# An attention and MLP block written out by a planner: first norm, Q lead, leftover cost, token order and bias row changed together

## The chip, the core and the metric

The kernel runs on one core of one Trainium2 chip. The metric is device time in microseconds (us). The core has five engines with queues of their own: PE (matrix multiply), DVE (vector), ACT (activation functions), POOL (general purpose) and SP, which here issues nearly all DMAs. Each engine works through its own instructions in the order in which the program lists them.

## The reference

One transformer block with modulation by a condition c, on 2048 tokens of width 512, with 32 heads of 16 columns and an MLP of width 1376:

```python
mod = (_silu(c) @ w_mod).reshape(c.shape[0], 6, 1, -1)      # sa, ca, ga, sb, cb, gb
h = _layernorm(x) * (1 + ca) + sa
q, k, v = split(h @ wqkv)                                   # 32 heads of 16
p = _softmax(q @ k.T * 16 ** -0.5)
x = x + ga * ((p @ v) @ wo)
h = _layernorm(x) * (1 + cb) + sb
x = x + gb * (_gelu(h @ w1 + b1) @ w2 + b2)
```

All inputs are bf16. The scores are 32 heads x 2048 x 2048 numbers, and each of them has to pass through an exponential: this is most of the work outside the matrix engine.

## The kernel before

**Blocks, runs and tiles.** Tokens are worked in four blocks of 512 (NQ, QB), each of four tiles of 128 (TPB). A head group is 8 heads, 128 columns of Q, K and V (index cc); the pair (b, cc) is a Q block with a head group. Attention is cut into 32 runs. A run handles four heads of one query block (in the last block, eight heads for half of the queries) and goes over 16 key tiles. A key tile of a run has four score units, one for each row group of 32 partitions of PE; a unit is 128x512 scores, made by one matmul in `qk` (L856). Two runs share one Q group; the Q tiles (`qm`) have four buffers.

**Two ways to the exponential.** ACT takes three or two units at a time from the PSUM tiles `st` and writes `pt` (L905). For up to four key tiles of each run (DKS; one in the first run) DVE takes the units instead, from the PSUM tiles `ax`: it writes score bits as 16-bit integers into `ph` (L946), which read as bf16 are a coarse exponential. Five readings with shifted bits, each against a V scaled to suit (VEB and the four VX of a tile), are added up by PE to refine it. The second to fourth readings are three adds on DVE (L962). The fifth, `shared_reading`, is four pieces; POOL takes as many as fit (L984), and DVE does the leftover in one instruction (L978) of 512 to 2048 columns. If a run's own tiles are used up, ACT takes from the tiles that DVE has not reached.

**Values.** `pv_op` (L1044) multiplies exponentials or readings with V and adds a run up in the PSUM bank `od`. After a run, `normalise` copies it out (L1069), and turns sums into reciprocals over small DMAs (dn, dc, rn, RB, issued on SP).

**The planner.** The order on every engine is written out by a planner in Python, before the program is built. Each piece of work is an `op` with an engine, a cost in us, what it depends on, a priority and at times a due point. `Plan.step` starts the piece that can start first; among those of an engine that can start nearly together it takes the lowest priority number, plus a small hashed amount (`spread`) that depends on the line or kind of the piece and on a seed, which changes every 25 us of planned time. Planned costs decide only the order; the hardware then goes by semaphores. When PE would have too little to do, the planner adds matmuls on zeros (L465, L470, L481) to keep it busy.

**Start.** SP issues the first x tile in two halves, two column blocks of w_mod, then (after the first of those has landed) the weight columns of the first head group, the other x tiles and the remaining columns. `layer_norm` works on DVE: statistics (`stats`, L641 and L642), POOL takes the power -1/2 (`rstd`, L646 and L648), DVE applies it (`apply`, L652), PE transposes (L694). In the first block the result is modulated as it is read from the PSUM tiles `st`, by DVE (L660) and ACT (L657). modA, the modulation, is made on PE from w_mod (L617) and finished on DVE (L630, L631). Then `make_q` (masked on DVE, L753), `make_k` (evicted by ACT, L665) and `make_v` (DVE, L667), with the projections at L735 and L774.

**Later Q groups.** `qk_deps` calls `want_q` whenever it lists a score matmul, and that makes the Q group needed next: four matmuls (L735), an eviction to `qs` on DVE (L757), and eight DMAs of 16 KB each, issued by SP (L763), that spread the heads into `qm`.

**Tails.** When the last run of a block is done, `block_tail` does the output projection, the second norm, W1, one tanh-approximated Gelu over the block on ACT (L1286, between two table loads) and W2 (L1210). The bias b2 is a row of the third part of W2 (`W2c`), met by rows of ones in `g`, which POOL writes after the Gelu (`ones`, L1217). W2 is scaled by the gate gb on POOL (L1119). The last block is done in halves; `last_half` follows the last exponential.

Of the kernel before, what the change touches and what calls it, by code (L numbers as in the profile page):

```python
# [11 lines left out]
ACT = mybir.ActivationFunctionType  # L12
# [51 lines left out]
SEEDS = (327, 149, 358, 994, 115, 625, 198, 230, 172, 718, 221, 116, 464, 544, 26, 159, 31, 414, 105, 313, 53, 464, 554, 383, 223, 329, 85, 286, 52, 14, 445, 498)  # L64
HEAT = 1.5

# [40 lines left out]
class Plan:  # L107
# [51 lines left out]
    def spread(self, o):  # L159
        x = ((sum(map(ord, o.kind)) if o.eng == "PE" else o.fn.__code__.co_firstlineno if o.fn else 0) * 2654435761 ^ SEEDS[min(int(self.now // 25.0), len(SEEDS) - 1)] * 2246822519) & 0xFFFFFFFF  # L160
        x = ((x ^ x >> 15) * 2246822519) & 0xFFFFFFFF
        return SPREAD * ((x ^ x >> 13) & 1023) / 1024.0
# [120 lines left out]
def kernel(  # L283
# [28 lines left out]
    EPS = 1e-5  # L312
    QSC = 0.25 * 128.0 / math.log(2.0)
# [95 lines left out]

    APR = 32  # L410
# [77 lines left out]
    x_src = A_x[0].rearrange("(b t p) d -> b p t d", t=TPB, p=P)  # L488
# [24 lines left out]
    def v_cols(v):  # L513
        return v[:, 0:32 * VW].rearrange("p (h w) -> p h w", w=VW)
# [8 lines left out]
    def load_x(b, deps=()):  # L523
        def go(o):
            nc.sync.dma_start(out=o.tile, in_=x_src[b])
        return dma(go, deps, kb=512, acq=r_xb, prio=0.0)
# [7 lines left out]
    for h in range(2):  # L534
        o_x0 += 2 * [dma(lambda o, h=h: nc.sync.dma_start(out=o_x[0].tile[:, 2 * h:2 * h + 2, :],
                                                         in_=x_src[0][:, 2 * h:2 * h + 2, :]),
                         (o_x[0],), kb=256, prio=0.0)]
    first = {}

    def load_mod(i):  # L540
        def go(o):
            first[i] = nc.sync.dma_start(out=o.tile, in_=wm_src[:, :, i * D:(i + 1) * D])
        return dma(go, kb=512, acq=r_blk, prio=0.01 + 0.01 * i)
    o_wm = {i: load_mod(i) for i in (0, 1)}

    def behind(i, load):
        tc.add_manual_dep(load.ins, first[i].ins.name, mybir.DependencyInfo(
            mybir.DependencyClass.Sync, mybir.DependencyReason.DATA), reason="order of loads")
    o_w, o_w0 = {}, {}
# [3 lines left out]
    def load_cols(i, lo, hi, prio):  # L553
        def go(o):
            got = nc.sync.dma_start(out=o_w[i].tile[:, :, lo:hi], in_=wq_src[:, :, i * D + lo:i * D + hi])
            if lo == 0 and i == 0:
                behind(0, got)
        return dma(go, (o_w[i], o_wm[0]), kb=(hi - lo) * (2 if lo == 0 else 1), prio=prio, n=2.7)
    o_w0 = {i: load_cols(i, 0, P, 0.1 + 0.01 * i) for i in range(3)}
    o_w1 = {}  # L560
    for b in range(1, NQ):
        o_x[b] = load_x(b, (o_wm[0],))
        o_x[b].prio = 0.2 + 0.1 * b
        o_w1[b - 1] = load_cols((1, 2, 0)[b - 1], P, D, 0.25 + 0.1 * b)
# [58 lines left out]
    def mod_columns(dst, ws, kind, warmer=True):  # L623
# [5 lines left out]
        def out_(o):  # L629
# [4 lines left out]
    o_mA = mod_columns(modA, [(o_wm[i], lambda i=i: o_wm[i].tile, o_wm[i]) for i in range(2)],  # L634
                       "modA", False)


# [6 lines left out]
    def rstd(ln, lo, hi):  # L644
        mv, rs = ln.tile
        nc.gpsimd.tensor_scalar(out=rs[:, lo:hi], in0=mv[:, lo:hi, 1], scalar1=EPS, scalar2=None,  # L646
                                op0=ALU.add)
        nc.gpsimd.tensor_tensor(out=rs[:, lo:hi], in0=rs[:, lo:hi], in1=mhalf[:, lo:hi], op=ALU.pow)  # L648
# [20 lines left out]
    def layer_norm(src, deps, mod, mod_dep, hold_z, alloc_h, engines, ps_res, kind, prio,  # L669
# [3 lines left out]
        st = [op("DVE", lambda o, t=t: stats(ln, t, src(t)), 0.83, (deps[t], ln, after and after[t]), prio=prio)  # L673
              for t in range(nt)]
        rs = [op("POOL", lambda o, i=i: rstd(ln, 2 * i, 2 * i + 2), 1.3,
# [49 lines left out]

    o_h = {}
# [7 lines left out]
    def proj(b, w, cc, kind, acq, after=None):  # L734
        return chain([(lambda ps, j=j: nc.tensor.matmul(  # L735
            out=ps[:, 0:QB], lhsT=w.tile[:, j, cc * P:(cc + 1) * P], rhs=o_h[b].tile[:, j, :],
            start=(j == 0), stop=(j == NC - 1)), MM) for j in range(NC)],
            [w, (o_w1 if cc else o_w0)[[o_w[i] for i in range(3)].index(w)], after] + (o_hd[b] if b else []), kind, acq, (o_h[b], w),
            need=None if b else lambda j: o_hd[b][j])

# [30 lines left out]
    def make_v(b, cc, kind, acq, eng, after=None):  # L771
# [14 lines left out]
        for t in DKS:  # L786
            if t // TPB == b:
                def scale(o, t=t):
                    for ph in range(1, NPH):
                        nc.gpsimd.tensor_scalar(  # L790
                            out=v_cols(VX[(t, ph)])[:, 8 * cc:8 * cc + 8, 0:16],
                            in0=v_cols(v_tile(t, 0))[:, 8 * cc:8 * cc + 8, 0:16], scalar1=PH_W[ph],
                            scalar2=0.0, op0=ALU.mult, op1=ALU.add)
                got.append(op("POOL", scale, 4 * 0.3, [got[0]] + o_vx0[t], prio=1.0, port=True))
# [66 lines left out]
    def qk_deps(r, kt):  # L861
        want_q(r // 2 + 1 if r < LAST * 8 else r - LAST * 4 + 2)
        cc, par, hb = run_heads(r)
        qm, evs = o_q[(cc, runs[r][0])]
        return [evs[par or 0], o_k[(cc, kt // TPB)]], qm
# [102 lines left out]
    def shared_reading(r, kt, first, es):  # L968
# [18 lines left out]
        def part(o):  # L987
            after_dve(add_pairs())
            n_piece[0] += 1
            if todo:  # L990
                done.todo += 1
            else:
                drop()
            o.waiters.append(done)
# [128 lines left out]
    def w2_scaled():  # L1123
        return scaled([lambda f=f: W2[f // 4].tile[:, f % 4, :] if f < 8 else W2c[:, f - 8, :] for f in range(NF)],
                      gb_bc, (W2[0], W2[1], o_late["small"], o_late["gb"]))
# [20 lines left out]
    def late_loads(after):  # L1146
# [11 lines left out]
        def wo(o):  # L1158
            nc.sync.dma_start(out=Wo, in_=A_wo.rearrange("(c p) f -> p c f", p=P))
            wo_src = A_wo[(NC - 1) * P:NC * P, :].rearrange("(r p d) f -> r p d f", r=4, p=2)  # L1160
            for r in range(4):
                for p in range(2):
# [4 lines left out]
                                   nc.gpsimd.memset(b1_bf, 0.0),  # L1167
# [48 lines left out]
    def ones(g, deps):  # L1216
        return op("POOL", lambda o: nc.gpsimd.memset(g.tile[FL:P, NF - 1, :], 1.0), 0.4, deps, prio=0.0)  # L1217
# [22 lines left out]
    def block_tail(b, nt=TPB):  # L1240
# [19 lines left out]
        if part:  # L1260
            g.uses += 1
            x2.uses += 1
            held["x"] = x2
            o_late["part"] = g
            one = ones(g, (g,))
# [19 lines left out]
        else:  # L1285
# [3 lines left out]
            one = ones(g, ge)  # L1289
# [17 lines left out]
    def store(b, t, a):  # L1307
        dma(lambda o: nc.sync.dma_start(
            out=out[0][b * QB + t * P:b * QB + (t + 1) * P, :], in_=a.tile), (a,), kb=128, rel=(a,))
# [94 lines left out]
    for b in range(NQ):  # L1404
        kind = f"in{b}"
        urgent.add(kind)
        o_h[b], o_hd[b], za, trs = layer_norm(
            lambda t, b=b: o_x[b].tile[:, t, :], o_x0 if b == 0 else [o_x[b]] * TPB, modA, o_mA, prev_tr, r_blk,
            ("DVE", "ACT") * 2 if b == 0 else ("DVE", "DVE", "ACT", "ACT") if b < 3 else ("DVE",) * 4, tuple(r_st[::-1]) if b == 0 else (r_ax, r_ax), kind, 0.6 + 0.2 * b, after)
# [8 lines left out]
        make_k(b, 0, kind, r_ax, "ACT")  # L1418
# [16 lines left out]
    def want_q(g):  # L1435
        while q_made[0] < g and q_made[0] + 1 < NQ * NC:
            q_made[0] += 1
            b, cc = groups[q_made[0]]
            due(32 + APR * (first_run(q_made[0]) - 1) - 32)
# [97 lines left out]
```

## Time and profile before

| what | value |
|---|---|
| runs | 781.15, 783.46, 783.68 us; median 783.46 |
| span of the profiled execution, first to last instruction | 782.9 us |
| first exponential (L905) starts | 14.79 us |
| ACT busy | 752.0 us, of which the exponentials 710.7 in 626 instructions |
| DVE busy | 722.6 us, of which the first readings (L946) 315.8 in 484 instructions |
| PE busy | 730.8 us |
| POOL busy | 256.6 us |
| DMA | 27.71 MB in 38547 packets, mean 35 GB/s |
| mean granted TensorE clock | 0.993 |

The time that the profiled execution took as a run is not listed beside its span; the span lies 0.56 us below the median of the runs, and within their spread. Times inside the profile count from the first instruction. A line such as L905 is a line of the kernel's source. "out<-in" gives the names of the tiles, and after the bar stand the busy time in us, the mean duration in ns, the idle time of the engine just before and what ended it.

### The profile page before, as it was taken

How to read it: one execution, taken by the hardware profiler on the slowest of the kernel's cores; microseconds unless marked ns; L12 is line 12 of the kernel's file. 1: busy time of each engine (PE TensorE's matmuls, PEld its weight loads, DVE VectorE, ACT ScalarE, POOL GpSimd, SP SyncE). 2: the span in 40 equal slices, each digit the busy share in tenths (PEclk: the TensorE clock that was granted, in tenths of full speed). 3: DMA queues.
4: the chain of work that ended last, by engine and by line, in shares of the span. 5: the costliest groups of instructions: out<-in, count | busy, mean ns of one | idle time of the engine just before them, and what ended most of it. 6: DMA issues, size and time to landing. Idle time of an engine off the chain costs nothing.

```text
span 782.9 us, 20900 instructions
## 1 busy us (share of the span) xinstructions
PE 730.8 (93%) x8315; PEld 271.3 (35%) x8395; DVE 722.6 (92%) x1269; ACT 752.0 (96%) x677; POOL 256.6 (33%) x492
## 2 busy tenths in 40 slices
PE   8889999999999999999999999999999999999997
PEld 3323333233333222233223233332333444444444
DVE  6789989999999999999999999999987999998984
ACT  4999999999999999999999999999999999999994
POOL 6620434333352534231313134234202432142320
PEclk9999999999999999999999999999999999999999
DMA  7043001100002001000101000000110000100000
GB/s 216 28 147 83 18 23 43 27 23 5 17 21 75 25 17 49 17 13 15 47 19 30 29 19 17 20 22 19 29 57 24 23 22 18 46 25 18 25 18 28
DMA packets 38547, 27.71 MB, mean 35 GB/s; under 512 B 17941, under 2 KB 33846, under 8 KB 38450
## 3 DMA queue, kind: packets, MB, share of 16 engines
q1 hardware_dynamic: 38442, 26.39, 11.8%
q8 instruction: 65, 1.06, 0.5%
q14 instruction: 32, 0.26, 0.1%
q10 hardware_dynamic: 8, 0.00, 0.0%
HBM read 20.77 MB, written 2.61 MB: 30 GB/s over the span
## 4 chain that ended last, share of the span: by engine, by line
ACT 37%; PE 34%; DVE 16%; issue 10%; DMA 2%; POOL 1%; SPq 0%; DVEq 0%; POOLq 0%; ACTq 0%
ACT pt L905 35%; PE od L1044 12%; PE st L856 10%; DVE ph L946 7%; DVE sh L962 4%; PE ax L1210 4%; PE ax L1271 3%; PE ax L856 2%; PE ax L735 1%; DMA blk<-in_w_mod_dram 1%; ACT g L1286 1%; PE t L1381 1%; DVE sh L978 1%; PE od L481 1%; DVE g L1276 1%
## 5 line engine op out<-in xcount | busy, mean ns | idle before, releaser
L905 ACT ACTIVATE pt<-st 128x1536 bf16<-128x1536 f32 x626 | 710.7, 1325 | 7.6 <-PE st L856 3.8
L946 DVE TENSOR_SCALAR ph<-ax 128x512 int16<-128x512 f32 x484 | 315.8, 681 | 25.3 <-PE ax L856 23.1
L856 PE MATMUL st<-qm,kT 32*128 32x512 bf16 x1564 | 246.4, 384 | 26.7 <-ACT pt L905 19.9
L962 DVE TENSOR_SCALAR sh<-ph 128x2048 int16<-128x2048 int16 x363 | 242.4, 700 | 2.0 <-PE od L1044 1.2
L984 POOL TENSOR_TENSOR sh<-ph,pair_sh 128x256 int32<-128x256 int32 x212 | 128.8, 616 | 280.6 <-DVE sh L962 190.4
L1044 PE MATMUL od<-sh,VX 128*32 128x512 bf16 (+1 forms) x2432 | 172.5, 342 | 1.7 <-DVE sh L962 0.7
L856 PE MATMUL ax<-qm,kT 32*128 32x512 bf16 x484 | 165.2, 380 | 7.3 <-DVE ph L946 4.3
L856 PEld LDWEIGHTS <-kT 32*128 32x128 bf16 x2048 | 79.4, 91 | 240.6 <-issue 228.7
L1044 PE MATMUL od<-pt,VEB 128*32 128x512 bf16 (+1 forms) x1952 | 142.7, 342 | 0.7 <-DVE OD L1069 0.5
L1044 PEld LDWEIGHTS <-VX 128*32 128x32 bf16 x2432 | 60.2, 96 | 82.7 <-issue 71.6
L1044 PEld LDWEIGHTS <-VEB 128*32 128x32 bf16 x2560 | 62.9, 96 | 73.5 <-issue 58.9
L1096 POOL TENSOR_TENSOR OT<-OD,RB 128x256 bf16<-128x256 f32 x38 | 29.0, 774 | 72.7 <-DVE sh L962 60.1
L978 DVE TENSOR_SCALAR sh<-ph 128x2048 int16<-128x2048 int16 (+3 forms) x86 | 50.7, 594 | 0.4 <-PE od L1044 0.3
L1044 PE MATMUL od<-ph,VEB 128*32 128x512 bf16 (+1 forms) x608 | 48.5, 341 | 0.4 <-DVE OD L1069 0.4
L1271 PE MATMUL ax<-blk,W 128*128 128x512 bf16 (+1 forms) x155 | 41.5, 352 | 1.7 <-issue 0.5
L1096 POOL TENSOR_TENSOR OS<-OD,RB 128x256 bf16<-128x256 f32 x24 | 17.5, 741 | 63.2 <-DVE sh L962 26.0
L790 POOL TENSOR_SCALAR VX<-VEB 128x128 bf16<-128x128 bf16 x64 | 23.4, 366 | 38.0 <-DVE VEB L667 34.8
L1210 PE MATMUL ax<-w,g 128*128 128x512 bf16 x115 | 32.4, 381 | 2.2 <-ACT g L1281 1.1
L735 PE MATMUL ax<-blk,w 128*128 128x512 bf16 x93 | 30.9, 383 | 2.8 <-ACT blk L657 0.6
L1276 DVE TENSOR_SCALAR g<-ax,b1c 128x512 bf16<-128x512 f32 (+1 forms) x44 | 29.3, 678 | 0.2
L641 DVE BATCH_NORM_STATS2 ln_s<-xb 128x6 f32<-128x512 bf16 x32 | 21.7, 678 | 1.8 <-DMA xb<-in_A_x_dram 1.7
L1210 PEld LDWEIGHTS <-g 128*128 128x128 bf16 x176 | 14.1, 97 | 24.5 <-issue 11.9
(109 smaller groups left out, 407.5 us busy)
## 6 DMA issues: line engine op xcount, KB each, us to landing
RB<-rn SPq DMA_DIRECT2D x124, 64.0 KB
xb<-in_A_x_dram SPq DMA_DIRECT2D x7, 512.0 KB
out_dram<-o SPq DMA_DIRECT2D x16, 128.0 KB
qm<-qs SPq DMA_DIRECT2D x120, 16.0 KB
W<-in_B_w_dram SPq DMA_DIRECT2D x1, 1376.0 KB
w<-in_A_wqkv_dram SPq DMA_DIRECT2D x3, 384.0 KB
blk<-in_w_mod_dram SPq DMA_DIRECT2D x2, 512.0 KB
g<-in_w_mod_dram SPq DMA_DIRECT2D x2, 512.0 KB
```

The source lines that it names most:

```text
L735: return chain([(lambda ps, j=j: nc.tensor.matmul(out=ps[:, 0:QB], lhsT=w.tile[:, j, cc * P:(cc + 1) * P], rhs=o_h[b].tile[:, j, :], start ...
L856: nc.tensor.matmul(out=o.tile[:, k * QB:(k + 1) * QB], lhsT=kT[cc][kb][rows, ko * P:(ko + 1) * P], rhs=qm.tile[rows, par, :] if hb is None ...
L905: nc.scalar.activation(out=e.tile[:, 0:len(got) * QB], in_=o.tile[:, 0:len(got) * QB], func=ACT.Exp, scale=ESC)
L946: nc.vector.tensor_scalar(out=ph.tile[:, o.row * QB:(o.row + 1) * QB], in0=o.tile, scalar1=PH_B, scalar2=0.0, op0=ALU.add, op1=ALU.max)
L962: sh = op("DVE", lambda o, j=j: nc.vector.tensor_scalar(out=o.tile, in0=first.tile, scalar1=PH_SH[j], scalar2=None, op0=ALU.add), 0.6, es, ...
L978: return nc.vector.tensor_scalar(out=sh.tile[:, at], in0=first.tile[:, at], scalar1=PH_SH[-1], scalar2=None, op0=ALU.add)
L984: return nc.gpsimd.tensor_tensor(out=sh.tile[:, at].bitcast(I32), in0=first.tile[:, at].bitcast(I32), in1=pair_sh[:, 0:1].to_broadcast([P, ...
L1044: nc.tensor.matmul(out=o_od[r].tile[32 * i:32 * i + 32, n * HB:n * HB + w], lhsT=v_tile(kt, ph)[:, c0:c0 + 32], rhs=got[i][:, at:at + w], ...
L1096: two = beside(lambda c: nc.gpsimd.tensor_tensor(out=OT.tile[:, c], in0=OD.tile[:, c], in1=o5.tile[:, c], op=ALU.mult), (OT,), (OD, o5), f ...
L1210: nc.tensor.matmul(out=ps, lhsT=g[:, f, col:col + P], rhs=rhs, start=(f == 0), stop=(f == NF - 1))
L1271: mm = chain([(lambda ps, f=f, j=j, f0=f0: nc.tensor.matmul(out=ps[:, (f - f0) * N:(f - f0 + 1) * N], lhsT=W1[:, j, f * P:(f + 1) * P], rh ...
L1276: ev.append(op("DVE", lambda o, f=f, f0=f0, mm=mm: nc.vector.tensor_scalar(out=g.tile[:, f, 0:N], in0=mm.tile[:, (f - f0) * N:(f - f0 + 1) ...
```

## The change

- **First norm** (`first_norm`, new): in the first block z is transposed before the modulation is known, in two parts (three tiles, then one). DVE and ACT copy it out of PSUM, and DVE modulates it in SBUF. The epsilon is added on DVE instead of POOL, in all four input norms. modA is summed in another order, row block by row block of w_mod.
- **Loads**: w_mod comes as four row blocks of 1024 columns instead of two column blocks of 512 columns; what follows waits for the second of them. The second x tile is issued ahead of the V columns. Planned transfer sizes (kb, which set planned landings only) are changed.
- **p-major tokens**: a partition holds four consecutive tokens, so that an x tile is read in rows of 4 KB; the output is stored to match.
- **Split K** (`split_k`, new): in the first two blocks K of the first head group is projected and evicted by ACT as 128 and 384 columns.
- **Q one group ahead**: `want_q` is asked for one group more, and the planned due point is 16 earlier (a run is 32).
- **Leftover by its size**: the planned cost of the DVE leftover is set anew each time that POOL takes a piece.
- **b2 for all tokens**: b1's padding is 8, so that the Gelu itself gives 8 in the padding rows; b2 is divided by 8 on POOL. Only the second half of the last block still has its rows set.
- **Planner**: VX scaling is four ops instead of one with four instructions; 64 seeds of 12.5 us instead of 32 of 25 us, with new values.

```diff
-SEEDS = (327, 149, 358, ...
+SEEDS = (318, 175, 812, ...
+STRETCH = 12.5
...
-        x = (... SEEDS[min(int(self.now // 25.0), len(SEEDS) - 1)] * 2246822519) & 0xFFFFFFFF
+        x = (... SEEDS[min(int(self.now // STRETCH), len(SEEDS) - 1)] * 2246822519) & 0xFFFFFFFF
...
-    x_src = A_x[0].rearrange("(b t p) d -> b p t d", t=TPB, p=P)
+    x_src = A_x[0].rearrange("(b p t) d -> b p t d", t=TPB, p=P)
+    out_dst = out[0].rearrange("(b p t) d -> b t p d", t=TPB, p=P)
...
-    def load_mod(i):
-        def go(o):
-            first[i] = nc.sync.dma_start(out=o.tile, in_=wm_src[:, :, i * D:(i + 1) * D])
-        return dma(go, kb=512, acq=r_blk, prio=0.01 + 0.01 * i)
-    o_wm = {i: load_mod(i) for i in (0, 1)}
+    def load_mod(j):
+        def go(o):
+            first[j] = nc.sync.dma_start(out=mod_cols(j), in_=wm_src[:, j, 0:2 * D])
+        return dma(go, (o_mod,), kb=250, prio=0.2 * j - 4.6)
+    o_wm = {j: load_mod(j) for j in range(NC)}
...
-            if lo == 0 and i == 0:
-                behind(0, got)
-        return dma(go, (o_w[i], o_wm[0]), kb=(hi - lo) * (2 if lo == 0 else 1), prio=prio, n=2.7)
-    o_w0 = {i: load_cols(i, 0, P, 0.1 + 0.01 * i) for i in range(3)}
+            if (lo, i) == (0, 0):
+                behind(1, got)
+        return dma(go, (o_w[i], o_wm[1]), kb=192 if lo == 0 else 340, prio=prio, n=1.2)
+    o_w0 = {i: load_cols(i, 0, P, (-3.0, -2.8, -2.4)[i]) for i in range(3)}
...
+        o_x[b] = load_x(b, (o_wm[1],))
+        o_x[b].prio = 0.5 * b - 3.1
...
+    def first_mod(ps, j):
+        for m in range(2 * NC):
+            nc.tensor.matmul(out=ps[:, m:m + 1], lhsT=mod_cols(j)[:, m * P:(m + 1) * P], rhs=sc[:, j:j + 1],
+                             start=(j == 0 and m == 0), stop=(j == NC - 1 and m == 2 * NC - 1))
...
+            if soon and t % 2:
+                plus_eps(nc.vector, ln, t - 1, t + 1)
...
+    def first_norm(kind):
...
+        def stat(t):
+            stats(ln, t, src(t))
+            if t > 1:
+                plus_eps(nc.vector, ln, 0 if t == 2 else t, t + 1)
...
+        rs = [op("POOL", lambda o, lo=lo, hi=hi: rstd(ln, lo, hi, True), 0.8, [st[hi - 1], o_mh], prio=0.0)
+              for lo, hi in ((0, 3), (3, 4))]
...
+                ev.append(op(e, lambda o, half=half, e=e, lo=lo, hi=hi, rows=rows, view=view: copy(
+                    e, h.tile[:, 2 * half:2 * half + 2, lo * P:hi * P], rows(view())),
+                    (0.07 if e == "DVE" else 0.23) + (hi - lo) * 0.267, (trs[-1], h), prio=0.3, rel=(banks[half],)))
...
+        mA = op("DVE", lambda o: nc.vector.tensor_tensor(out=modA, in0=mm.tile[:, 0:2 * NC], in1=plus, op=ALU.add),
+                0.2, [mm, ev[2]] + o_plus, lat=0.03, prio=0.0, rel=(mm,))
+        done = [op("DVE", lambda o, j=j: modulate("DVE", h.tile[:, j, :], h.tile[:, j, :], modA, j), 0.21,
+                   [mA] + ev[j // 2::2], prio=0.05, port=True) for j in range(NC)]
...
+    def split_k(b, kind):
+        evs = []
+        for lo, hi in ((0, P), (P, QB)):
+            mm = chain([(lambda ps, j=j, lo=lo, hi=hi: nc.tensor.matmul(
+                out=ps[:, 0:hi - lo], lhsT=o_w[1].tile[:, j, 0:P], rhs=o_h[b].tile[:, j, lo:hi],
+                start=(j == 0), stop=(j == NC - 1)), MM * (hi - lo) / QB) for j in range(NC)],
+                [o_w[1], o_w0[1]], kind, r_ax, (o_h[b], o_w[1]), need=lambda j: o_hd[b][j])
+            evs.append(op("ACT", lambda o, mm=mm, lo=lo, hi=hi: copy("ACT", kT[0][b][:, lo:hi], mm.tile[:, 0:hi - lo]),
+                          0.2 + 0.3 * (hi - lo) / QB, (mm,), prio=0.3, rel=(mm,)))
+        o_k[(0, b)] = evs[1]
+        o_k0[b * TPB] = evs[0]
...
-        want_q(r // 2 + 1 if r < LAST * 8 else r - LAST * 4 + 2)
+        want_q(r // 2 + 2 if r < LAST * 8 else r - LAST * 4 + 3)
...
-            due(32 + APR * (first_run(q_made[0]) - 1) - 32)
+            due(32 + APR * (first_run(q_made[0]) - 1) - 48)
...
         def part(o):
             after_dve(add_pairs())
             n_piece[0] += 1
+            q.us = 0.067 + 0.1333 * len(todo)
...
+        b2 = op("POOL", lambda o: nc.gpsimd.tensor_scalar(
+            out=W2c[FL:P, 2, :], in0=W2c[FL:P, 2, :], scalar1=1.0 / ONE, scalar2=0.0, op0=ALU.mult, op1=ALU.add), 1.2,
+            (o_late["small"],), prio=2.0)
...
-                                   nc.gpsimd.memset(b1_bf, 0.0),
+                                   nc.gpsimd.memset(b1_bf, ONE),
...
-            one = ones(g, ge)
+            one = None
```

## Prediction

> **What bounds the kernel now.** I read the page's busy shares, costliest groups and chain first, then the activity by stretches, then the chain of waits of the first 16 us, and last the waits of single engines.
>
> ```profile
> PE 730.8 (93%) x8315; PEld 271.3 (35%) x8395; DVE 722.6 (92%) x1269; ACT 752.0 (96%) x677; POOL 256.6 (33%) x492
> ...
> L905 ACT ACTIVATE pt<-st 128x1536 bf16<-128x1536 f32 x626 | 710.7, 1325 | 7.6 <-PE st L856 3.8
> L946 DVE TENSOR_SCALAR ph<-ax 128x512 int16<-128x512 f32 x484 | 315.8, 681 | 25.3 <-PE ax L856 23.1
> ```
>
> L905 is the exponential on ACT, L946 the first reading of a score tile that DVE takes instead. A score unit is one 128x512 piece. There are 2048: 32 runs of 16 key tiles, 4 units each. DVE took 484, which is 121 tiles, and ACT the other 1564. An ACT unit cost 710.7 / 1564 = 0.454 us, a tile of four 1.82 us. At most 125 tiles may go to DVE (4 in each of 31 runs, 1 in the first), so four that DVE could have taken went to ACT. That is 7.3 us of ACT.
>
> ```profile
> 0.00:14.79 14.79, 12.17 (x95) 5.75 (x96) 8.20 (x23) 3.80 (x6) 10.17 (x44) 1.00 0.73 215
> 14.79:45.00 30.21, 25.53 (x230) 11.45 (x233) 22.03 (x51) 27.84 (x28) 14.84 (x62) 0.94 0.18 57
> 45.00:305.00 260.00, 242.84 (x2609) 83.75 (x2630) 250.25 (x428) 258.75 (x229) 99.93 (x179) 1.00 0.15 42
> ...
> 583.00:596.00 13.00, 12.15 (x189) 5.40 (x190) 6.97 (x12) 12.21 (x12) 1.70 (x2) 1.00 0.13 37
> ```
>
> Each row gives length, then busy time of PE, PEld, DVE, ACT and POOL. From 45 us on ACT is full: 258.75 of 260. So whatever moves the first exponential, at 14.79, or takes work or a stall from ACT moves the end, and nothing else in the middle does. After the last exponential, near 760, come 22.9 us that no edit shortens.
>
> The stretch 583:596 is the odd one. DVE is busy for 6.97 of 13, and its own rows show why:
>
> ```profile
> 586.11 1.89 DVE L962 TENSOR_SCALAR sh<-ph 128x2048 int16<-128x2048 int16 x3
> 592.45 0.69 DVE L946 TENSOR_SCALAR ph<-ax 128x512 int16<-128x512 f32 x1 [4.45 <-PE ax L856]
> ```
>
> PE waited there up to 0.99 us for the DMA qm<-qs. The Q of the next head group was evicted at 585.5 and its eight copies went out from 586.2 to 593.8. DVE lost 4.45 us, ACT 0.79.
>
> Start, from the chain of waits:
>
> ```profile
> 2.23 6.80 DMA blk<-in_w_mod_dram
> 9.03 0.05 issue
> 9.08 0.55 PE ax L617 x16
> 9.63 0.71 PE st L694 x12
> 10.34 0.03 issue
> 10.36 0.56 DVE blk L660
> ```
>
> w_mod lands at 9.03, transposes end at 10.34, DVE and ACT modulate out of PSUM in turn (second ACT piece to 12.39), q is projected by 12.81, k evicted by 14.31, first exponential 14.79.
>
> **The sum, part by part.** It is made against the profiled span, 782.9 us. The three runs had a median of 783.46, 0.56 above it; I carry that over.
>
> *First norm.* It turns z before w_mod counts, copies out of PSUM, then modulates in SBUF on DVE. x lands as before (first statistics at 3.62, four end at 6.92). Two small additions of epsilon join DVE, 0.18 each by row L631, to 7.28. POOL's power after the third tile (0.78) ends near 7.0, so three z at 0.40 (L652's usual duration) end at 8.48, the fourth at 8.88. Six transposes per bank: about 0.45, the DVE bank near 8.95. Copies of 768 and 256 columns: L660's 0.537 at 512 and 0.340 at 128 make 0.51 ns a column, so 0.67 and 0.40, to 10.05. Add of modA 0.17. Four modulations: the nearest row is L652, same form, SBUF to SBUF; 0.40 each, to 11.8. Last q matmul to 12.2, against 12.81. Then the masked Q (0.70) ends at 12.95. Split K (128 columns: 0.3 for its matmuls, about 0.33 for its copy, between L611's 0.17 and L665's 0.63) is ready just before, so k no longer ends last. Scores 0.42: first exponential 13.45, which is **-1.35**. Bounds: with L978's 0.283 at 512 columns for the modulation and x 0.4 sooner, -2.3; if POOL's memsets delay its power and PE waits in order behind pieces planned too short (the planner charges 0.21 for a modulation), -0.3.
>
> The Trainium skill, in VectorE: DVE Perf Modes, section on the TRN2 errata, gives SBUF-to-SBUF work on VectorE 58 + FD/Accel cycles at 0.96 GHz. My estimate from it is (58 + 128) / 0.96 = 0.19 us for a modulation, the first exponential 0.8 us earlier still; L652 has a mean of 0.445 at that form and a fastest of 0.38, so the trace disagrees and the row decides.
>
> *Split K in two blocks*: two more ACT evictions. Cover after the first exponential is gone, since ACT is full; block 1's first scores may come sooner, in the waits of 0.46 and 0.49 around 24.7 to 25.75. +0.4 to -0.4; I take **+0.15**.
>
> *p-major tokens and loads.* Rows of 1 KB become 4 KB in x, 2 KB in w_mod (four loads for two). DMA ran at 215 GB/s up to 14.79, but at 409 in 57:59, where longer rows moved: w_mod could land up to 1.7 us sooner. By the working above DVE ends last, not w_mod, so **0**; if w_mod landed no sooner it would still precede the copies' end. q, k and the second x tile are released by the second w_mod load, not the first of two, and need not leave DMA nearly idle from 7 to 9 us (103 GB/s). SP issues two more loads at 0.5 each, hidden while data flows; uncovered, +1.0. DVE is not free for the second tile before 13, so earlier landing only lets that block move with the first. Stores keep 1 KB rows: 0.
>
> *Q one group ahead.* No instruction is added; each group's four matmuls, eviction (0.68) and eight issues (about 5 us of SP) come some 44 us (two runs) earlier. On SP they pass normalisation's dn, dc, rn and RB transfers, whose product only the tails read: 0 while that cover holds, up to 5 us on a run's normalisation if not. On DVE they pass score tiles. It takes away the stall at 592: **-0.8** on ACT, and frees 4.45 us on DVE. Bounds 0 and -1.5.
>
> *Leftover by its size.* The instructions stay; only the planner's clock of DVE changes.
>
> ```profile
> L978 DVE TENSOR_SCALAR sh<-ph 128x1024 int16<-128x1024 int16 x15 | 6.4, 426 | 0.0
> ```
>
> These are the leftovers of half a tile: 15 of them, 0.426 each. Three quarters came 27 times at 0.582, one quarter 5 times at 0.283, a full one takes 0.707, and the plan charged all alike. It thought DVE 27 x 0.125 + 15 x 0.281 + 5 x 0.424 = 9.7 us busier than it was. A DVE tile costs 4 x 0.65 + 3 x 0.67 + 50.7 / 121 = 5.0 us. 9.7 + 4.45 makes 2.8 tiles; whole ones reachable, I take two of the four: 2 x 1.82 = **-3.6**. DVE can bear it (busy 682 of 715 us in the stretches from 45 to 760). Bounds 0 and -7.3. Each moved tile adds four readings of some 0.22 us on PE; PE also has filler matmuls to give up.
>
> *b2 for all tokens.* Three POOL memsets (0.52 to 1.09 us) between the activation of a block and its W2 matmuls go; one scaling of W2c comes (nearest row L1119, 0.68), hidden on a POOL busy 33%; uncovered it costs 0.7 once, ahead of W2. ACT spends the freed moments on its table load (1.28) anyway, which is what is late next: **0**, bounds -1 and +0.7.
>
> *New tie-breaks (seeds of 12.5 us).* They re-deal the order; the trace cannot show how. 0, with 2 us each way from the stalls at 310 and 321 below.
>
> Sum: -1.35 + 0.15 - 0.8 - 3.6 = -5.6. 782.9 - 5.6 = 777.3, plus 0.56: **777.9 us**.
>
> **The rivals.** *Everything is recovered*: all four tiles go to DVE (-7.3), the start gains 2.3, and the two stalls where PE ran at half clock vanish with the Q stall (-2.2 - 0.8). 782.9 - 12.6 + 0.56 = 770.9. For it:
>
> ```profile
> 304.15:307.57 3.42, 2.14 (x27) 1.00 0.03 2
> 307.57:310.98 3.41, 3.41 (x31) 0.50 0.28 77
> ```
>
> A stretch in which PE was busy for 2.14 of 3.42 us is followed by one at a granted clock of 0.50 (the number after the count); the same comes once more, 2.51 busy up to 317.81, then 0.50. ACT waited 0.81 + 0.16 in the first, 1.24 in the second. A re-dealt order may feed PE there. Against it: four of four is the ceiling. [...]
>
> *Start and stall only*: the tiles stay with ACT, since DVE lags for other reasons. -1.35 + 0.15 - 0.8 = -2.0: 781.5, within the noise. It includes the change not doing what it says, with loads or plan landing where they were (783). For it: DVE is 94 to 98% busy from 100 to 300, where two tiles were lost.
>
> *DVE loses tiles, slower*: Q brought two runs forward falls between 45 and 165 us on the k and v of the next heads. DVE is fullest there, and a run can never give back a tile later, having at most four. Each costs ACT 1.82. From -2.0, three tiles more than now on ACT (1576 units) make it slower; four give +5.3: 788.8. Against: Q evictions are 0.68 each, a seventh of a tile, and only three groups lie there.
>
> **Chances and range.** Forecast 0.56, everything 0.24, start only 0.09, slower 0.11. Below 0.3% (2.35 us) a measurement of this kernel cannot tell a change. So faster 0.80, same 0.09, slower 0.11. The range runs from 770.0, just past the full recovery, to 783.5, start-only without its gains; slower is left out. The forecast alone spans 775 to 780.7 (three tiles and a start of -2.3; one tile and -0.3).
>
> **What would show it.** First L905 near 13.45, split K ending before the masked Q; L946 count 492 (two tiles) with 1556 units on ACT; no DVE gap above 2 us waiting for scores at a head border and no PE wait on qm<-qs; three fewer memsets of g. Wrong if L946 stays at 484 or falls, if the first exponential is after 14.4, or if the granted clock shows 0.50 in more than three stretches before the tail.

## The result and the profile after

The changed kernel took 785.66 us (median of 17 runs, 784.64 to 786.5), the kernel before 783.19 beside it (781.07 to 784.57). The ratio is 1.0029, with a 95% interval of 1.002 to 1.0039: 2.5 us slower, where 5.6 us faster was forecast and 770.0 to 783.5 was the range. That is about the 0.3% which the prediction took as the limit of what a measurement can tell.

The profiled execution of after took 786.0 us, with a span of 784.2, which is 1.8 us less; the later runs show 1.7 to 2.3. The span of 782.9 before therefore belongs to an execution of about 784.7 us (an estimate), at the slow end of its runs, and not 0.56 below the median as the prediction had it. So the two profiles differ by 1.3 us only and the medians by 2.5; the profiles can account for the 1.3. Medians are given throughout, since single runs lie far above the others of their kernel (two of a1_nofill's twelve by 7 us, one of b_lo's at 915.79 us, which its ratio leaves out).

Busy time, then the two groups that share the score units between ACT (L989, L905 before) and DVE (L1030, L946 before), from the page of after:

```profile
PE 734.3 (94%) x8290; PEld 273.0 (35%) x8370; DVE 729.4 (93%) x1290; ACT 751.8 (96%) x677; POOL 256.5 (33%) x491
...
L989 ACT ACTIVATE pt<-st 128x1536 bf16<-128x1536 f32 x624 | 711.1, 1297 | 7.6 <-PE st L940 4.7
L1030 DVE TENSOR_SCALAR ph<-ax 128x512 int16<-128x512 f32 x488 | 318.7, 683 | 15.1 <-PE ax L940 13.6
```

DVE has 488 first readings for 484, one tile more, and ACT 1560 units for 1564. Yet ACT's exponentials are busy for 711.1 us against 710.7, and idle before them for 7.6 as before. One tile should have taken 1.8 us away.

I split each run at the first exponential's start and the last one's end. Before: 14.79 us, then 745.20, then 22.87. After: 16.20, then 745.05, then 22.95. The start lost 1.4 us, and the middle gained nothing.

The activity by stretches of after has the same layout as before:

```profile
0.00:16.20 16.20, 14.67 (x100) 6.94 (x102) 9.92 (x29) 3.58 (x8) 9.60 (x45) 1.00 0.80 251
16.20:45.00 28.80, 25.84 (x240) 12.07 (x241) 24.32 (x60) 27.94 (x29) 15.26 (x63) 1.00 0.11 32
45.00:305.00 260.00, 243.46 (x2586) 83.13 (x2606) 248.14 (x424) 258.01 (x228) 104.59 (x180) 0.99 0.15 42
```

PE is busy for 14.67 of the first 16.20 us. That is the key to the start, as the chain of waits shows (start, length, what):

```profile
8.31 0.58 PE ax L648 x24
8.89 0.24 PE od L473
9.13 0.22 PE ax L468
...
10.44 0.22 PE ax L468
10.66 0.35 PE st L778 x6
11.01 0.02 issue
11.03 0.57 DVE blk L684
...
12.88 1.38 DVE blk L677 x4
14.26 0.61 DVE ln_s L654
14.87 0.02 issue
14.89 0.18 DVE mv L655
15.07 0.65 DVE qm L837
...
16.20 1.45 ACT pt L989
```

L468 and L473 are the filler matmuls on zeros. Eight of them stand in PE's queue between 8.89 and 10.66, ahead of the transposes L778. What the transposes need was there well before 10.66, as the timeline says:

```profile
7.55 1.50 DVE L669 TENSOR_SCALAR z<-xb,mv,rs 128x512 bf16<-128x512 bf16 x4 [0.31 <-POOL rs L665]
...
11.03 0.56 DVE L684 COPY blk<-st 128x768 bf16<-128x768 bf16 x1 [1.97 <-PE st L778]
```

z is complete at 9.05; DVE then idles 1.97 us for the transposes.

### The profile page after: what moved, and what is told of

Same layout as the page of the kernel before. It is cut to its first block, busy times and chain, and to the rows that moved or that the text cites. A ratio compares the mean times of both kernels' runs of the same rounds, so it can differ in the third digit from the quotient of the medians.

```text
span 784.2 us, 20871 instructions
## 1 busy us (share of the span) xinstructions
PE 734.3 (94%) x8290; PEld 273.0 (35%) x8370; DVE 729.4 (93%) x1290; ACT 751.8 (96%) x677; POOL 256.5 (33%) x491
## 4 chain that ended last, share of the span: by engine, by line
PE 34%; DVE 27%; ACT 26%; issue 9%; DMA 2%; SPq 1%; POOL 0%; DVEq 0%; ACTq 0%; POOLq 0%
ACT pt L989 24%; DVE ph L1030 13%; PE od L1129 12%; PE st L940 9%; DVE sh L1046 8%; PE ax L1298 4%; PE ax L940 2%; PE ax L1359 2%; DMA dc<-dn 2%; PE ax L805 1%; DVE sh L1062 1%; ACT g L1374 1%; DVE g L1364 1%; DVE OD L1154 1%; PE ax L468 1%
## 5 line engine op out<-in xcount | busy, mean ns | idle before, releaser
L989 ACT ACTIVATE pt<-st 128x1536 bf16<-128x1536 f32 x624 | 711.1, 1297 | 7.6 <-PE st L940 4.7
L1030 DVE TENSOR_SCALAR ph<-ax 128x512 int16<-128x512 f32 x488 | 318.7, 683 | 15.1 <-PE ax L940 13.6
L1046 DVE TENSOR_SCALAR sh<-ph 128x2048 int16<-128x2048 int16 x366 | 246.4, 704 | 0.8 <-PE od L1129 0.2
L1068 POOL TENSOR_TENSOR sh<-ph,pair_sh 128x256 int32<-128x256 int32 x219 | 131.7, 611 | 299.1 <-DVE sh L1046 216.5
L940 PE MATMUL ax<-qm,kT 32*128 32x512 bf16 x488 | 167.0, 380 | 7.1 <-DVE ph L1030 4.3
L873 POOL TENSOR_SCALAR VX<-VEB 128x128 bf16<-128x128 bf16 x64 | 25.9, 405 | 20.9 <-DVE VEB L684 17.5
L805 PE MATMUL ax<-blk,w 128*128 128x512 bf16 x89 | 29.3, 382 | 2.8 <-DVE ph L1030 1.5
L1298 PEld LDWEIGHTS <-g 128*128 128x128 bf16 x176 | 14.7, 97 | 26.1 <-issue 12.5
L654 DVE BATCH_NORM_STATS2 ln_s<-xb 128x6 f32<-128x512 bf16 x32 | 21.8, 682 | 1.3 <-DMA xb<-in_A_x_dram 1.2
```

The source lines that it names most:

```text
L805: return chain([(lambda ps, j=j: nc.tensor.matmul(out=ps[:, 0:QB], lhsT=w.tile[:, j, cc * P:(cc + 1) * P], rhs=o_h[b].tile[:, j, :], start ...
L940: nc.tensor.matmul(out=o.tile[:, k * QB:(k + 1) * QB], lhsT=kT[cc][kb][rows, ko * P:(ko + 1) * P], rhs=qm.tile[rows, par, :] if hb is None ...
L989: nc.scalar.activation(out=e.tile[:, 0:len(got) * QB], in_=o.tile[:, 0:len(got) * QB], func=ACT.Exp, scale=ESC)
L1030: nc.vector.tensor_scalar(out=ph.tile[:, o.row * QB:(o.row + 1) * QB], in0=o.tile, scalar1=PH_B, scalar2=0.0, op0=ALU.add, op1=ALU.max)
L1046: sh = op("DVE", lambda o, j=j: nc.vector.tensor_scalar(out=o.tile, in0=first.tile, scalar1=PH_SH[j], scalar2=None, op0=ALU.add), 0.6, es, ...
L1068: return nc.gpsimd.tensor_tensor(out=sh.tile[:, at].bitcast(I32), in0=first.tile[:, at].bitcast(I32), in1=pair_sh[:, 0:1].to_broadcast([P, ...
```

## The experiments

Each edit keeps the line numbers of its kernel unless it says otherwise, since the tie-breaks (`spread`) hash the line number of the code. "Middle" is from the first exponential's start to the last one's end; "ACT units" are of 2048. Both are from the one profiled execution of each.

### Eight fillers less, nothing else (e1_nofill)

```diff
-            return Op("PE", lambda o: nc.tensor.matmul(
+            return Op("PE", lambda o: skip() or nc.tensor.matmul(
...
-    pv_run = [None]
+    pv_run = [None]; n_fill = [0]; skip = lambda: (n_fill.__setitem__(0, n_fill[0] + 1), 22 <= n_fill[0] <= 29)[1]
```

The planner still plans the eight (their zeros are read by nothing); they are not issued. All else keeps its order.

> The changed kernel with eight matmuls on zeros left out that stand on PE ahead of the first transposes (8.76 to 10.28 us in its trace); the order of everything else is unchanged. Theory (the fillers hold the transposes back): transposes start near 8.9 instead of 10.49, the first exponential near 14.75 instead of 16.20, the time falls by 1.4 us, to about 784.2 and a ratio to the kernel before of 1.0013. Rival (the transposes wait for z, or the copies out of PSUM are what ends last): the first exponential stays within 0.3 us of 16.2 and the ratio at 1.003.

Measured: 783.77 us (781.72 to 784.7), ratio 1.0006 (0.9994 to 1.0018), 1.9 us below after. Its chain of waits:

```profile
8.29 0.58 PE ax L648 x24
8.87 0.37 PE st L778 x6
...
12.50 0.61 DVE ln_s L654
...
13.32 0.65 DVE qm L837
...
14.44 1.45 ACT pt L989
```

The first exponential moved from 16.20 to 14.44: 1.76 us, and the eight took 1.77 in the queue. The two executions show full clock from nearly the same moment (5.83 and 5.88 us), so the pair is a clean one. It settles what held the transposes: not DVE, not w_mod, not POOL, but fillers in PE's in-order queue.

### The deal of the tie-breaks (b_shift1, b_shift2, b_shift3, a_shift1, a_shift2, a_shift3)

One, two or three empty lines near the top change every line number, so ties fall otherwise; no work, planned cost or seed is changed. The order that comes of it is called a deal here. What the planner decides on the way changes with it: which engine takes a unit, and how many fillers it adds.

> The kernel before with one empty line put into its source ahead of the planner. No instruction's work, cost or seed changes, but the hash that breaks ties takes the line number of an operation, so every tie of DVE, ACT, POOL and SP is dealt anew. Theory (the deal itself is worth as much as the parts of the change, and the seeds of before suit only its own lines): slower than before by 2 to 6 us, other counts of L946 units. Rival (the deal is worth little): within 0.15% of before, that is 1.2 us.

> The changed kernel with one empty line put into its source ahead of the planner: only the ties are dealt anew. Theory (the deal is worth several us, and the new seeds suit the changed kernel's own lines): 787 to 792 us. Rival (the new seeds suit nothing in particular): as likely faster as slower, within 2 us of 785.7.

> The kernel before with two empty lines put in near the top: every line number is two higher and so the tie-breaks are dealt once more, nothing else. If the deal of before was a lucky one, which one other deal says (791.05), this is slower again, 785 to 792, and before's own 783.2 is at the fast end of what its code gives; if that one deal was an accident of its start (17.5 us to the first exponential), this one stands within 1.5 us of before.

> The kernel after with two empty lines: a third deal of the kernel after, whose first two gave 785.7 and 782.4. If the change itself is worth some 2 to 5 us and its own deal was unlucky, this stands at 781 to 784, below the deals of before; if the change is worth nothing, it falls anywhere from 781 to 791 as the deals of before do. First exponential between 14.8 and 16.2 in either case, as the fillers ahead of the transposes are still there.

> The kernel before with three empty lines, a fourth deal. If the deal of before was a lucky one, 786 to 800 again; the other reading, that two bad deals were chance, gives 782 to 786.

> The kernel after with three empty lines, a fourth deal; so far 785.7, 782.4 and 789.1. If the change is worth some us that the deals hide, this is in 781 to 790 again, and lower than the fourth deal of before; if it is worth nothing, it may as well be 791 to 800.

| kernel | median us | ratio to before (95%) | first exponential | middle | ACT units |
|---|---|---|---|---|---|
| before | 783.19 | 1 | 14.79 | 745.20 | 1564 |
| b_shift1 | 791.05 | 1.0106 (1.0082 to 1.0129) | 17.51 | 746.31 | 1568 |
| b_shift2 | 803.43 | 1.0266 (1.0244 to 1.0288) | 17.47 | 759.00 | 1576 |
| b_shift3 | 789.80 | 1.0083 (1.0057 to 1.0109) | 17.22 | 747.86 | 1572 |
| after | 785.66 | 1.0029 (1.002 to 1.0039) | 16.20 | 745.05 | 1560 |
| a_shift1 | 782.42 | 0.9999 (0.9981 to 1.0017) | 15.26 | 743.13 | 1564 |
| a_shift2 | 789.07 | 1.0081 (1.0058 to 1.0103) | 15.31 | 750.96 | 1568 |
| a_shift3 | 783.11 | 1.0006 (0.9982 to 1.003) | 15.62 | 741.36 | 1560 |

The ratios are to the runs of before that were taken beside each kernel (medians of 782.3 to 783.2), so they are not quotients of the first column. An empty line moves before by 7 to 20 us and after by 3 us each way. The prediction had priced this at 0 with 2 each way. Before's own deal is by far the best of its four: in the three others the first x tile is issued behind w_mod, and the first exponential comes 2.4 to 2.7 us later. After's own deal is the third of its four.

### No tie-breaks at all (b_sp0, a_sp0), and the old seeds (a_oldseed)

```diff
-SPREAD = 0.15
+SPREAD = 0.00
```

In a_oldseed the seeds of before, 25 us each, stand in the kernel after.

> The kernel before with SPREAD = 0, so that no seed and no line number decides between operations that are nearly due; the rest is the same. If before's own deal is a lucky one, this is slower than 783.2, near the mean of its three deals (783.2, 791.1, 803.4: 792). If deals only scatter by 2 us, as the prediction took it, 781 to 785.

> The kernel after with SPREAD = 0. The comparison with the kernel before at SPREAD = 0 leaves out the deal. If the change is worth what the prediction's surviving terms give (the stall for Q gone, one or two more tiles on DVE, less the late start of 1.4 us), this is 1 to 7 us faster than before at SPREAD = 0. If the parts give nothing and only the deals differ, the two stand within 1.5 us of one another, or this one 1 to 2 us later by its start.

> The kernel after with the seeds of before, one for 25 us: the part of the change that lists new tie-breaks undone by itself. The prediction priced it at 0 +-2: 783.7 to 787.7. If it is a deal like an empty line, it falls where the deals of after fell, 782 to 789, or up to the 788 of no tie-break at all; and if the new seeds are a lucky deal for the change, as before's were for before, it is slower than after.

Measured: b_sp0 788.66 us, ratio 1.0077 (1.005 to 1.0104); a_sp0 788.18, ratio 1.0069 (1.0041 to 1.0096); a_oldseed 784.53, ratio 1.0018 (1.0007 to 1.003). Without any deal the two kernels cannot be told apart. a_oldseed lies among the deals of after, 1.1 us below after's own: it is a deal like the others, and the new seeds are no gain by themselves. The groups of a_sp0, then of b_sp0, show how:

```profile
L989 ACT ACTIVATE pt<-st 128x1536 bf16<-128x1536 f32 x626 | 711.7, 1310 | 12.1 <-PE st L940 6.0 <-PE ax L940 5.6
L1030 DVE TENSOR_SCALAR ph<-ax 128x512 int16<-128x512 f32 x484 | 315.5, 682 | 24.9 <-PE ax L940 22.1 <-PE st L940 1.4
```

```profile
L905 ACT ACTIVATE pt<-st 128x1536 bf16<-128x1536 f32 (+1 forms) x631 | 715.8, 1327 | 5.2 <-PE st L856 2.3 <-PE ax L856 1.5 <-PE od L1044 0.8
L946 DVE TENSOR_SCALAR ph<-ax 128x512 int16<-128x512 f32 x472 | 308.8, 683 | 27.7 <-PE ax L856 26.3
```

With the change DVE takes three tiles more (484 against 472) and ACT's exponentials need 4.1 us less. But ACT waits 12.1 us for them instead of 5.2, and the first comes at 15.64 instead of 14.64. In these two executions a_sp0 had four 3.41 us windows at a granted clock of 0.50 in the middle, b_sp0 none.

### Single parts (b_lo, b_q, a_noq)

b_lo puts only the leftover's size into the kernel before (`q.us = 0.067 + 0.1333 * len(todo)` in `part`), b_q only the Q group one ahead; a_noq takes that lead out of after:

```diff
-        want_q(r // 2 + 2 if r < LAST * 8 else r - LAST * 4 + 3)
+        want_q(r // 2 + 1 if r < LAST * 8 else r - LAST * 4 + 2)
...
-            due(32 + APR * (first_run(q_made[0]) - 1) - 48)
+            due(32 + APR * (first_run(q_made[0]) - 1) - 32)
```

> The kernel before with the DVE leftover charged by its size alone, on the same lines and with the same seeds. By the prediction's term: one or two tiles more on DVE (488 or 492 units in L946) and 1.8 to 3.6 us faster. Rival (a planned cost alone only deals the order anew): tile count up or down by one or two, time within the spread that an empty line gives (782 to 791), not faster than 781.

> The kernel before with Q one group ahead alone (one group more asked for, due point 16 earlier), on the same lines and with the same seeds. By the prediction's term: no wait on the Q copies near 592, a stall of 0.8 us gone, one tile more on DVE (488 units), 1 to 3 us faster. Rival (what it takes away is given back by the new order): the stall at 592 is gone, yet the time lies at or above 783.2, with stalls elsewhere.

> The kernel after with the Q of a head group made one group later again, as in the kernel before; nothing else is changed and no line moves. If making Q ahead is what eats the gain (its eviction and eight transfers pass DVE's tiles and the normalisation), this kernel is faster than after by 1 to 3 us (about 783), the stall for Q near 592 is back at 1 us or less of ACT, and DVE has 123 or more tiles. If the Q lead is worth its -0.8, it is slower than after by about 1 us (786.5). Since this too re-deals the rest of the order, two to three us either way without a change in the tiles would be the deal and not the Q.

Measured: b_lo 783.17 us, ratio 1.0003 (0.9989 to 1.0016), and exactly the 121 tiles of before. b_q 784.93, ratio 1.0025 (1.0015 to 1.0035): the stall at 592 is gone, and DVE has two tiles fewer (119). a_noq 796.18, ratio 1.017 (1.0143 to 1.0196): 10.5 us slower than after, with 119 tiles instead of 122 (5.5 us of ACT) and the stall back. From its chain of waits, then from its windows:

```profile
586.01 1.79 DMA qm<-qs
...
587.87 3.51 DMA qm<-qs
```

```profile
590.37:593.78 3.41, 2.27 (x33) 0.76 (x33) 2.08 (x4) 2.32 (x3) 0.79 (x2) 1.00 0.20 58
593.78:597.20 3.42, 3.20 (x17) 0.66 (x17) 2.95 (x6) 2.42 (x3) 1.16 (x2) 0.50 0.00 0
597.20:600.61 3.41, 3.15 (x35) 1.11 (x33) 1.55 (x4) 2.05 (x2) 0.72 (x1) 0.50 0.02 6
```

PE is short of work while the Q transfers land, and then runs two windows at half clock (the number after the last count), in which ACT is busy for 4.5 of 6.8 us. So a Q stall costs more than its wait; b_cap below has the same picture, a wait of 2.4 us and then two such windows. But b_lo, b_q and a_noq are new deals too, and the last two disagree: the lead alone made before slower, its removal made after slower. The profiled execution of b_q also ran at half clock from 10.49 to 13.91 us, and its first exponential came at 16.08. What the lead is worth cannot be read from these two. That it is worth several us is not excluded: a_noq lies above all six orders of after that have the lead (782.42 to 789.07), and b_q below every order of before but its own (788.66 to 803.43).

### ACT's work and the clock (b_cap, a_nozero)

b_cap offers DVE three tiles instead of four in runs 7, 11, 17 and 21 of before. a_nozero leaves out every filler that after plans between 60 and 740 us.

```diff
-    shared = [[kt for kt in (DKS if r else FIRST_DKS)] for r in range(NR)]
+    shared = [[kt for kt in ((DKS[:3] if r in (7, 11, 17, 21) else DKS) if r else FIRST_DKS)] for r in range(NR)]
```

```diff
-            return Op("PE", lambda o: nc.tensor.matmul(
+            return Op("PE", lambda o: 60 < plan.now < 740 or nc.tensor.matmul(
...
-        for i in range(4):
+        for i in range(0 if 60 < plan.now < 740 else 4):
```

> The kernel before with DVE offered three instead of four key tiles in the four runs 7, 11, 17 and 21: ACT gets 16 units more (1580), on the same lines and seeds. Theory of the prediction (ACT's work sets the length of the middle, a tile is worth 1.82 us): first to last exponential 745.2 + 7.3 = 752.5, time near 790. Rival (what ACT gains by handing over a tile comes back as waits for scores, so the tile is worth little): the middle within 2.5 us of 745.2, ACT's idle time and the late starts of its exponentials fall by several us, time 782 to 786.

> The changed kernel without the matmuls on zeros between 60 and 740 us of planned time (129 in its trace, 124 of them in groups of four that run side by side, some 7 us of PE); the order of all other work is unchanged. Theory (PE is what makes exponentials late in the middle): ACT's waits fall and the middle shortens by 1 to 4 us, to 741 to 744 from 745.05. Rival (the fillers keep the granted clock up and stand in time that PE has): more stretches at 0.50 than the one of 128.8 to 132.2, and the middle stays or grows.

Measured: b_cap 793.56 us, ratio 1.0143 (1.0122 to 1.0164). It ended with three tiles fewer (118), not four, and its middle is 8.0 us longer: 5.5 by three tiles at 1.82; two windows at 0.50 from 589.5 fall into the rest. This is one deal as well, but the twenty profiles together agree with it: the middle has a mean of 745.3 us in the five kernels with 1560 units on ACT and of 753.2 in the three with 1576, which is 2.0 us for a tile. So the tiles were the right currency. a_nozero took 791.51, ratio 1.0109 (1.0089 to 1.013). Its windows say why:

```profile
113.25:116.66 3.41, 1.52 (x15) 0.50 (x15) 1.70 (x3) 3.41 (x5) 0.00 (x0) 1.00 0.00 0
116.66:137.14 20.48, 19.93 (x147) 4.81 (x147) 14.37 (x28) 15.63 (x13) 8.18 (x13) 0.50 0.15 41
```

PE has little to do in the first row, and the clock drops. It then stays at 0.50 for 20.5 us, although PE is busy for 19.93 of them, and ACT for 15.63 only; why it stays is not shown. Between 60 and 740 us a_nozero spends 30.7 us at half clock, after 3.4. In this order the fillers of the middle earn their place; the eight of the start do not.

### The same fillers out in other deals (a1_nofill, a2_nofill, a3_nofill)

The same eight fillers left out of a_shift1, a_shift2 and a_shift3.

> The changed kernel with the empty line (a_shift1: 782.4 us, first exponential 15.26) and without the same eight matmuls on zeros ahead of the first transposes; the rest of its order is as in a_shift1. Theory (the fillers are a fixed delay of the start, whatever the deal): first exponential 13.5 to 13.9, the time falls by 1.5 to 1.9 us, to about 780.7, which is under the kernel before by 0.3%. Rival (with fewer fillers the granted clock falls to 0.50 in the start, as in b_q): no gain, 782 or more.

> The third deal of after (two empty lines), and of its filler matmuls the same eight ahead of the first transposes left out (their values are used nowhere); otherwise the same order. If the fillers hold the transposes, the first exponential is 0.4 to 1.9 us sooner than in the same deal with them, and the time lower by as much, as in the two pairs already run (-1.9 and -1.1 us). If their work for the granted clock matters more, the start shows full clock later and the gain is gone.

> The fourth deal of after (three empty lines, 783.1, the one with the shortest middle, 741.4 us) less the eight filler matmuls ahead of the first transposes. If these hold the transposes in every deal, the first exponential moves from 15.62 to 14.1 to 14.9 and the time falls by 0.7 to 1.5, to 781.6 to 782.4, just under the kernel before; if the granted clock decides the start instead, it stays at 783.

Measured: 781.28 us, ratio 0.9994 (0.9969 to 1.0019); 788.49, ratio 1.0077 (1.0049 to 1.0104); 780.96, ratio 0.9978 (0.9966 to 0.9991). Their first exponentials are at 14.79, 14.34 and 14.34, sooner than with the fillers by 0.47, 0.97 and 1.28. The first pair is not clean: the records show full clock from 5.84 us in a1_nofill and from 3.96 in a_shift1, and the last section shows that a late moment delays a start with fillers. In the other two pairs the moments lie within 0.06 us. The medians fall by 1.1, 0.6 and 2.2, of which the second is within the scatter. a3_nofill is the only kernel of the study whose interval lies below before's time, and by less than that limit of 0.3%; that its deal was picked out of four must be counted against it.

## Why the prediction was wrong, point by point

**First norm, -1.35; measured +1.4.** The step that failed is the one from z to the transposes. The prediction lets them follow at once ("Six transposes per bank: about 0.45, the DVE bank near 8.95"). Its bound of -0.3 named PE waiting in order, but for pieces planned too short, and was set far too small: the eight fillers cost 1.77 us by the pair of chains above. Even without them the first exponential was at 14.44, not 13.45. That last microsecond has two pieces in e1_nofill. The second copy and modA came late: the fourth tile's transposes waited 0.3 for DVE's first copy, two more fillers went ahead of the last piece of modA, and modA ended at 11.09 instead of 10.22. Then DVE's statistics of the second block (L654 and L655, 12.50 to 13.32) went ahead of the masked Q; the sum had said that they would not fall before 13. The last of Q's matmuls ended at 12.93, so of these 0.8 us some 0.4 counted. In between, the modulation was shorter than forecast, 1.38 us for four (0.345 each) against 0.40. The estimate of 0.19 from the Trainium skill (VectorE: DVE Perf Modes, TRN2 errata) is refuted by this too: the form measured nearly twice that. The same section says itself that its row comes out too low for a single operation.

The +1.4 is itself the difference of one execution each. b_lo and b_cap have the same order up to the first exponential as before, a_nozero the same as after, and they gave 14.14 and 14.65, and 15.29. So the loss lies between 0.5 and 2.1 us, by the moment at which the clock became full and, in before, at which w_mod landed.

**Leftover by its size, -3.6: the term that decided the forecast.** The reasoning was that the planner thinks DVE 9.7 us busier than it is and will hand over tiles when told the truth. b_lo tells it, and the count stayed at 121. So the step that failed is the one from planned time to tiles: in this order the planned time of DVE is not what withheld the four. The orders of before hold 118 to 121 tiles, so that a tile or two in another order is not excluded. What withheld the four stays open.

**Q lead, -0.8.** The mechanism held: after shows no PE wait on qm<-qs at 592. Over all runs, PE's waits for qm<-qs between 17 and 757 us came to 0.2 us or less in eleven of the twelve kernels with the lead (1.0 in a_sp0), and were above 0.2 in six of the eight without it, up to 3.4. The size failed: ACT's idle time in the middle stayed (8.09 before, 7.96 after), since other waits took its place. One was priced at 0 as long as its cover held, normalise's transfers behind Q's on SP:

```profile
DVE dc L1165 <- DMA dc<-dn: 4.2, 6, 1.1
```

That is 4.2 us in six waits, where before had 0.6 in two. It isn't the lead's alone: without it this wait ranges from 0.2 to 3.4 over the deals. How much of the 4.45 us that DVE was to win went there is not shown. DVE's waits for scores did fall, from 23.1 to 13.6 us, and DVE took one tile more.

**New tie-breaks, 0 with 2 each way.** This was the largest error of size. Between successive exponentials, the starts of after are 19.8 us later in sum than at the shortest steps (1.330 us behind three units, 0.903 behind two), those of before 16.5. In the other orders of after it runs from 14.2 (a_oldseed) to 22.9 (a_sp0), in those of before from 13.9 (b_sp0) to 25.4 (b_shift2), with means of 18.2 and 17.7 over all. So the 1.8 us of the one tile gained were used up by many small late scores, 3.3 us more than before's own deal had, and ties alone move this sum by more than that. The middle came to -0.1 that way.

**Split K, p-major, b2: taken as +0.15, 0 and 0.** None of them was tested alone, and the profile shows no cost of theirs. The first 128 columns of K are out at 15.21, before the masked Q, as forecast. PE has no wait on w_mod. The tail is 22.95 against 22.87.

**The rivals.** "DVE loses tiles" had the right side and the wrong mechanism: after has a tile more. "Everything is recovered" fell, though its half-clock stretches at 307 and 318 did vanish; another came at 128.76. Such stretches belong to an execution as well as to an order: e1_nofill, with after's order, has one from 125.30 that is twice as long. The rival that was missing is the one that happened: the start is held by PE's queue, and the order of the middle is dealt anew, from a kernel whose own deal is the best of its five.

**What the change is worth apart from the deal.** Averaged over its deals and the run without ties, before is at 791.2 us (five kernels), after at 785.5 (six, with a_oldseed), and ACT has 1571 and 1563 units. That fits two tiles and an earlier start (the first exponential at 16.33 and 15.76 on average). But the spread is as large as the difference, the one comparison without ties shows none, and no single part was seen to bring the tiles. It stays open. The difference of 5.7 us is close to the 5.6 of the forecast, and as far as these runs show that is luck.

## What to carry to other kernels

Where a generator writes the order, an edit is also a new draw among orders: move a line number or a seed of both versions and see the spread before a few microseconds are ascribed to an edit. When work is moved earlier on one engine, read what is queued on the next engine at that moment, fillers too; being ready at 9.05 is worth nothing behind 1.8 us of zeros. And a difference between planned and real cost is only worth what the planner would do with it: test that alone, since it costs one line.

## What the runs showed of the hardware

**The start follows the phase of the clock.** With the fillers in place, the first exponential of after's code follows the moment from which the records show full clock in that execution: full from 3.96, 4.02, 4.06, 4.70, 4.73, 5.88, 6.59 and 6.69 us, exponential at 15.26, 15.29, 15.31, 15.62, 15.64, 16.20, 16.55 and 16.59 (a_shift1, a_nozero, a_shift2, a_shift3, a_sp0, after, a_oldseed, a_noq). a_nozero, after, a_oldseed and a_noq have one and the same order up to there, so that between them only the clock differs. Each microsecond at half clock costs half a microsecond, because PE's queue is full of fillers: 0.427 us each at 0.50, 0.215 at full clock. Without the eight it depends far less on that moment: 14.34, 14.34, 14.44 and 14.79 at 3.99, 4.64, 5.83 and 5.84 (a2_nofill, a3_nofill, e1_nofill, a1_nofill). That part of the spread of the runs comes from this is likely, but was not measured. The Trainium skill (TensorE: Matmul & The Clock Gate, Part 1) says that the window runs freely and the moment varies from run to run; these traces agree.

**Even a window that is mostly busy may be followed by half clock.** The same section gives an idle window of about 3.4 us as what brings the clock down, and tells beside it of a kernel in which many short pauses of PE did. An idle window does not explain these traces: windows that were mostly busy were followed by 0.50, and the busy share alone does not tell which. From the windows of after:

```profile
125.35:128.76 3.41, 2.93 (x32) 0.92 (x35) 3.38 (x11) 3.41 (x5) 2.65 (x4) 1.00 0.04 12
128.76:132.17 3.41, 3.41 (x35) 0.60 (x31) 2.58 (x5) 2.70 (x4) 1.73 (x3) 0.50 0.19 65
```

PE was busy for 2.93 of 3.41 us, and half clock followed; in a_noq a window with 2.86 busy, from 586.96, was followed by full clock. What tells the two apart was not measured.
